# A one-core decode block: the last V loaded earlier, all heads treated alike, the MLP's inner products as rows, and W_down in row blocks

## The chip, the cores and the metric

The kernel runs on one core of one Trainium2 chip. The metric is the device time of one execution in microseconds (us), as a median over several executions. Below, DVE is the vector engine, ACT the scalar engine, PE the matmul engine, PEld its weight loads, POOL the GpSimd engine, and SP the engine that issues most DMA transfers.

A profile shows one execution. Its span runs from the first to the last instruction and is about 2 us shorter than the device time of the same execution. Times within a profile are us from the span's start.

## The reference, cut to what matters

Two rows of 512 numbers go through a layer norm, an attention block with one query per row against a cache, a residual, another layer norm and a gated MLP with a residual.

```
x: 2 x 1 x 512      K, V cache: 2 x 32 heads x 8192 x 128 (bf16)
q = layernorm(x) @ wq;  p = softmax(q . K / sqrt(128));  o = p @ V
h  = x + o @ wo                                  # wo: 4096 x 512
n  = layernorm(h)
y  = h + (relu(n @ W_gate) * (n @ W_up)) @ W_down   # F = 1376
```

The cache is 268 MB of the 281 MB that the kernel reads, and each byte of it is used once.

## The kernel before: the parts that matter

Four heads make a quad. There are 16 quads; quad 15 is the last. DVE multiplies K by the query and adds up the products, ACT takes the exponentials, and PE multiplies the weights by V. K has two buffers, V has one. After the loop, all remaining weights go into the K buffer that quad 14 leaves:

```python
for n in range(N - 1):
    scores(n, ...)
    if n + 2 < N: load_k(n + 2)
    collect(); ...; weighted_v(n)
    if n + 2 < N: load_v(n + 1)
W = kring.tile([P, RING], bf16, tag="k", name="W")
# ... cut: wo_sb, wol, wgu, wd_sb are views of W
for k, n in enumerate(SIZES): ...                # load wo
CUTS = (0, T // 2, T * 7 // 8, T * 15 // 16, T)
load_v(N - 1, CUTS)                              # then the last V
# ... then gate, up, W_down in blocks of 128 rows, and 96 rows last
```

The last quad takes a road of its own. The first seven eighths of its V are summed as rows and the last eighth as columns (`v_stationary`). Its sums come out as columns (one head after another), go into a small multiply, and join the rest of the attention row, which has been multiplied by `wo` beforehand:

```python
o_sum = lanes_of(o15)                            # DVE: four masked steps
v_stationary(N - 1, o_b, CUTS[2], CUTS[3])
nc.tensor.matmul(out=o_b, lhsT=o_sum, rhs=lane_of[:, 0, :], ...)
v_stationary(N - 1, o_b, CUTS[3], T)
normalize_last(L, o_b, zil)
for h in range(G):
    project(wol[:, h, :], ol[:, h, :], last=(h == G - 1))
hc = a_ps + xc                                   # (as code: one DVE add)
mu = centred(hc, "ln2");  hd = hc - mu           # (shortened)
mlp_in(0, gate_ps)       # 44 matmuls of 2 columns: the weights are loaded, hd moves
var = variance(hd_f, "ln2")
mlp_in(1, up_ps)         # 44 more
# ... cut: relu, product; then 44 matmuls of 128 columns with W_down; y_row; two output DMAs
```

The softmax here doesn't subtract the row's maximum and nothing guards it: scores larger than these inputs give would overflow.

Of the kernel before, what the change touches and what calls it, by code (L numbers as in the profile page):

```python
# [17 lines left out]
def kernel(  # L18
# [13 lines left out]
    nc = tc.nc  # L32
# [38 lines left out]
    zm = consts.tile([P, B, NQ - 1], f32)  # L71
    zl = consts.tile([P, B, G], f32)
# [6 lines left out]
    nc.vector.memset(eps_t, EPS)  # L79
    nc.vector.memset(mean_c, 1.0 / D)  # L80
    nc.vector.memset(zm, 0.0)
    nc.vector.memset(zl, 0.0)
    nc.vector.memset(row_of, 0.0)
    ident = consts.tile([P, P], bf16)
    masks.make_identity(nc, ident)
    zero = consts.tile([P, 1], bf16)
    nc.gpsimd.memset(zero, 0.0)
    nc.gpsimd.memset(pm, 0.0)

    SIZES = (4, 2, 1)  # L90
    FIRST = (0, 4, 6)
# [3 lines left out]
    half_blk = consts.tile([P, 2], f32)  # L95
    pick = {n: consts.tile([P, Q // n], f32, name=f"pick{n}") for n in SIZES}
    spread = {n: consts.tile([P, min(n, 2), G, Q // n], f32, name=f"spread{n}") for n in SIZES}
    same = {n: consts.tile([P, n, G, Q // n], f32, name=f"same{n}") for n in SIZES}

    def build_masks():  # L100
        def red(out, in_, axis=AXIS.X):
            nc.vector.tensor_reduce(out=out, in_=in_, axis=axis, op=ALU.add)

        red(turn_of, ident.rearrange("p (g t h) -> p t g h", t=TG, h=G), AXIS.XY)
        red(lane_of, ident.rearrange("p (g u t h) -> p u h g t", u=2, t=TG, h=G), AXIS.XY)
        red(head_blk, ident.rearrange("p (h m) -> p h m", h=G))
        red(half_blk, ident.rearrange("p (u m) -> p u m", u=2))
        red(row_of[:, 0:B], ident.rearrange("p (g q) -> p q g", q=Q)[:, 0:B, :])
        for n in SIZES:
            u = min(n, 2)  # L110
            red(pick[n], ident.rearrange("p (h m) -> p m h", m=Q // n))
            nc.vector.tensor_copy(spread[n], _view(lane_of, 0, [[G, u], [1, G], [0, Q // n]]))
            nc.vector.tensor_copy(same[n], _view(head_blk, 0, [[0, n], [1, G], [0, Q // n]]))
# [7 lines left out]
    x_row = opool.tile([B, D], bf16, tag="row")  # L121
# [6 lines left out]
    def centred(hc, pfx):  # L128
# [5 lines left out]
        return mu.unsqueeze(1).to_broadcast([P, KC, B])  # L134
# [13 lines left out]
    for c in range(KC):  # L148
# [5 lines left out]
    nc.vector.tensor_tensor(out=xd, in0=xc, in1=centred(xc, "ln1"), op=ALU.subtract)  # L154
# [3 lines left out]
    xn = misc.tile([P, KC, B], bf16)  # L158
    nc.vector.tensor_tensor(out=xn, in0=xd, in1=rstd.unsqueeze(1).to_broadcast([P, KC, B]),
                            op=ALU.mult)  # L160
    xnb = opool.tile([P, KC, B, Q], bf16, tag="row")
    nc.vector.tensor_copy(xnb, xn.unsqueeze(3).to_broadcast([P, KC, B, Q]))
    nc.scalar.activation(out=warm, in_=xn[0:1, 0, 0:1], func=ACT.Exp)
# [3 lines left out]
    qrep = consts.tile([P, B, NQ, Dh], bf16)  # L167
# [25 lines left out]
    LQ = NQ - 1  # L193
# [21 lines left out]
    def scores(n, cuts=(0, T)):  # L215
# [4 lines left out]
        for lo, hi in zip(cuts[:-1], cuts[1:]):  # L220
# [10 lines left out]
            nc.vector.tensor_reduce(out=sc[:, lo:hi], in_=kp[:, :, 0:8], axis=AXIS.X, op=ALU.add)  # L231
        for h in range(G):
            ps = slice(h * Q, (h + 1) * Q)
            nc.scalar.activation(out=p_of[ps, :, :, h],  # L234
                                 in_=sc[ps, :].rearrange("p (g t) -> p g t", t=TG), func=ACT.Exp,
                                 accum_out=(zm[ps, b, i:i + 1] if i < LQ else zl[ps, b, h:h + 1]),
                                 scale=SCALE)
# [3 lines left out]
    NK = sum(SIZES) * J  # L241
    oc = misc.tile([P, NK, B], bf16)
    ol = misc.tile([P, G, B], bf16)
    ou = misc.tile([P, NK], f32)
    reps, pair = {}, {}

    def clear(o):

        nc.tensor.matmul(out=o, lhsT=_view(zero, 0, [[0, P]]), rhs=_view(zero, 0, [[0, TG * Dh]]),
                         start=True, stop=False, skip_group_check=True)  # L250
# [12 lines left out]
    def lanes_of(o):  # L263

        osb = opool.tile([P, Dh], f32, tag="row", name="osb")
        nc.vector.tensor_scalar_mul(osb, o[:, 0:Dh], turn_of[:, 0:1])  # L266
        for t in range(1, TG):
            nc.vector.scalar_tensor_tensor(out=osb, in0=o[:, t * Dh:(t + 1) * Dh],  # L268
                                           scalar=turn_of[:, t:t + 1], in1=osb,
                                           op0=ALU.mult, op1=ALU.add)  # L270
        return osb

    def place(i):
        k = max(a for a in range(len(SIZES)) if FIRST[a] <= i)
        return k, i - FIRST[k]

    def weighted_v(n):
        b, i = seq[n]
        k, u = place(i) if i < LQ else (None, 0)
        paired = i < LQ and SIZES[k] > 1  # L280
        if not paired or u % 2 == 0:
            pair["o"] = ps_o.tile([P, TG * Dh], f32, tag="o", name="o")
        o = pair["o"]
        lane = u % 2 if paired else 0
        done = lane == 1 or not paired
        v_moving(n, o, 0, T, lane, first=(lane == 0), last=done)
        pair["done"] = (o, b, i) if done else None

    def collect():

        if not pair.get("done"):
            return
        o, b, i = pair.pop("done")
        osb = lanes_of(o)
        if i == LQ:
            o_l = ps_s.tile([P, G], f32, tag="st", name="o_l")
            nc.tensor.matmul(out=o_l, lhsT=osb, rhs=lane_of[:, 0, :], start=True, stop=True)  # L297
            nc.vector.tensor_copy(ol_f, o_l)  # L298
            return
        k, u = place(i)  # L300
        where = 0 if k == 0 else 1
        if u // 2 == 0 and k < 2:
            reps[where] = ps_acc.tile([P, 2, Dh], f32, tag=f"rep{where}", name="rep")
        n_of = SIZES[k]
        at = (u // 2) * 2 * (P // n_of)
        m = min(n_of, 2) * (P // n_of)
        nc.tensor.matmul(out=reps[where][at:at + m, max(k - 1, 0), :],  # L307
                         lhsT=spread[n_of].rearrange("k u h m -> k (u h m)"),
                         rhs=osb, start=True, stop=True, skip_group_check=True)

    def gather(k):

        n_of = SIZES[k]
        j, m = J * n_of, Q // n_of
        r = reps[0 if k == 0 else 1][:, max(k - 1, 0), :]
        at = FIRST[k] * J
        nc.vector.tensor_tensor(out=r.rearrange("p (m j) -> p m j", j=j),  # L317
                                in0=r.rearrange("p (m j) -> p m j", j=j),
                                in1=_view(pick[n_of], 0, [[1, m], [0, j]]), op=ALU.mult)
        nc.vector.tensor_reduce(out=ou[:, at:at + j], in_=r.rearrange("p (m j) -> p j m", j=j),  # L320
                                axis=AXIS.X, op=ALU.add)

    def v_stationary(n, o, lo, hi):
        vt = vts[n]
        for t in range(lo, hi):
            nc.tensor.matmul(out=o, lhsT=vt[:, t, :], rhs=p_of[:, t // TG, t % TG, :],
                             start=(t == CUTS[2]), stop=(t == T - 1), skip_group_check=True)

    def sum_z(zb, lhsT, z):
        nc.tensor.matmul(out=zb, lhsT=lhsT, rhs=z, start=True, stop=True)  # L330
        return zb

    def row_z(b, zb):
        for k, n in enumerate(SIZES):
            sum_z(zb[:, FIRST[k]:FIRST[k] + n], same[n].rearrange("p u h m -> p (u h m)"),
                  zm[:, b, FIRST[k]:FIRST[k] + n])
        return zb

    def last_z(b, zb):

        return sum_z(zb, mean_f, zl[:, b])

    def z_tile():
        return ps_s.tile([P, LQ + G], f32, tag="st", name="zb")

    def normalize(b, zb):
        zs = misc.tile([P, 6], f32, name=f"zs{b}")
        nc.vector.tensor_tensor(out=zs[:, 0:4], in0=zb[:, 0:4], in1=head_blk, op=ALU.mult)
        nc.vector.tensor_tensor(out=zs[:, 4:6], in0=zb[:, 4:6], in1=half_blk, op=ALU.mult)
        zi = misc.tile([P, 3], f32, name=f"zi{b}")  # L350
        nc.vector.tensor_reduce(out=zi[:, 0:1], in_=zs[:, 0:4], axis=AXIS.X, op=ALU.add)
        nc.vector.tensor_reduce(out=zi[:, 1:2], in_=zs[:, 4:6], axis=AXIS.X, op=ALU.add)
        nc.vector.tensor_copy(zi[:, 2:3], zb[:, 6:7])
        nc.vector.reciprocal(out=zi, in_=zi)
        for k, n in enumerate(SIZES):
            at = FIRST[k] * J
            nc.vector.tensor_scalar_mul(oc[:, at:at + n * J, b], ou[:, at:at + n * J],  # L357
                                        zi[:, k:k + 1])

    def invert_last(b, zb):  # L360
        zi = misc.tile([P, G], f32, name=f"zil{b}")
        nc.vector.reciprocal(out=zi, in_=zb)
        return zi

    def normalize_last(b, o, zi):
        nc.vector.scalar_tensor_tensor(out=ol[:, :, b], in0=o, scalar=1.0 / D,
# [202 lines left out]
```

## Time and profile before

| what | value | where it is read |
|---|---|---|
| time | 661.11 us (three runs, 661.11 to 661.63) | timed runs |
| DVE busy | 609.6 us of 659.4 (92%) | page, part 1 |
| HBM read | 281.06 MB, 426 GB/s over the span | page, part 3 |
| scores of quad 15 end | 631.86 | chain of waits |
| V's row sums (its first seven eighths) taken up | 645.75 | timeline |
| last V matmul (of the last eighth) ends | 648.12 | timeline |
| centred row `hd` starts | 650.12 | timeline |
| y matmuls start; y_row starts | 654.38; 656.09 | timeline |

These lines are from the page of the kernel before: busy time by engine, then for 40 equal slices of the span the DMA engines' busy share in tenths (9 is 90% or more) and the GB/s moved.

```profile
PE 119.5 (18%) x1341; PEld 58.6 (9%) x1341; DVE 609.6 (92%) x225; ACT 55.8 (8%) x142; POOL 2.5 (0%) x8
...
DMA  9999999999999999999999999999999999999996
GB/s 382 445 445 445 395 433 446 437 445 418 417 445 437 441 442 398 445 445 426 441 417 433 445 422 441 437 417 441 426 441 441 421 438 426 433 441 433 393 420 259
```

The DMA engines are busy for 90% or more of every slice but the last. DVE is nearly as long. So the body is a stream. That leaves the tail after the last scores. The chain of waits for it, followed back from the last instruction (start, duration, engine, tile written, source line):

```profile
629.57 2.29 DVE sc L231
...
639.53 2.49 PE o L257 x32
...
644.34 1.31 PE o L257 x24
...
650.12 0.17 DVE hd L493
...
654.38 1.17 PE y_ps L466 x31
...
656.09 0.29 DVE y_row L535
```

There is no DMA in this chain, in the pieces that are cut here either: from 631.86 to 656.09, 24.23 us, the tail is bound by compute. The traffic meanwhile ends earlier, as the windows of 1 us show (length; busy time and count on PE, PEld, DVE, ACT and POOL; granted PE clock as a share of full speed; DMA share; GB/s; a transfer's packet is counted in the window in which it starts, so a share can pass 1):

```profile
651.00:652.00 1.00, 1.00 (x30) 1.00 (x28) 0.00 (x0) 0.00 (x0) 0.00 (x0) 0.50 1.06 425
652.00:653.00 1.00, 1.00 (x23) 1.00 (x23) 0.42 (x4) 0.00 (x0) 0.00 (x0) 0.50 0.90 320
653.00:654.00 1.00, 1.00 (x29) 0.97 (x27) 0.15 (x2) 0.00 (x0) 0.00 (x0) 0.50 0.51 166
654.00:655.00 1.00, 0.67 (x21) 0.45 (x24) 0.24 (x2) 0.00 (x0) 0.00 (x0) 0.50 0.08 30
```

### The profile page before, as it was taken

How to read it: one execution, taken by the hardware profiler on the slowest of the kernel's cores; microseconds unless marked ns; L12 is line 12 of the kernel's file. 1: busy time of each engine (PE TensorE's matmuls, PEld its weight loads, DVE VectorE, ACT ScalarE, POOL GpSimd, SP SyncE). 2: the span in 40 equal slices, each digit the busy share in tenths (PEclk: the TensorE clock that was granted, in tenths of full speed). 3: DMA queues.
4: the chain of work that ended last, by engine and by line, in shares of the span. 5: the costliest groups of instructions: out<-in, count | busy, mean ns of one | idle time of the engine just before them, and what ended most of it. 6: DMA issues, size and time to landing. Idle time of an engine off the chain costs nothing.

```text
span 659.4 us, 3234 instructions
## 1 busy us (share of the span) xinstructions
PE 119.5 (18%) x1341; PEld 58.6 (9%) x1341; DVE 609.6 (92%) x225; ACT 55.8 (8%) x142; POOL 2.5 (0%) x8
## 2 busy tenths in 40 slices
PE   2100302003030210303012130301202030020446
PEld 1000101001010100101001110100001010010225
DVE  2899999999999999999999999999999998999952
ACT  2201001010101001010101001010010101001020
POOL 1000000000000000000000000000000000000000
PEclk9555755757565575756557575555757555575656
DMA  9999999999999999999999999999999999999996
GB/s 382 445 445 445 395 433 446 437 445 418 417 445 437 441 442 398 445 445 426 441 417 433 445 422 441 437 417 441 426 441 441 421 438 426 433 441 433 393 420 259
DMA packets 7314, 281.26 MB, mean 427 GB/s; under 512 B 802, under 2 KB 1412, under 8 KB 2308
## 3 DMA queue, kind: packets, MB, share of 16 engines
q1 hardware_dynamic: 7272, 281.06, 98.9%
q8 instruction: 10, 0.16, 0.1%
q14 instruction: 4, 0.03, 0.0%
q10 hardware_dynamic: 28, 0.01, 0.0%
HBM read 281.06 MB, written 0.00 MB: 426 GB/s over the span
## 4 chain that ended last, share of the span: by engine, by line
DVE 62%; DMA 33%; PE 3%; issue 1%; ACT 0%; DVEq 0%
DMA k<-in_A_k_cache_dram 31%; DVE k L222 29%; DVE k L228 28%; DVE sc L231 4%; DMA wq_sb<-in_A_wq_dram 2%; DVE osb L268 1%; DVE qrep L188 1%; PE qps L175 1%; PE o L257 1%; PE ar_ps L452 0%; ACT qrep L186 0%; PE y_ps L466 0%; PE a_ps L459 0%; PE gate_ps L510 0%; PE up_ps L510 0%
## 5 line engine op out<-in xcount | busy, mean ns | idle before, releaser
L222 DVE TENSOR_TENSOR k<-k,qrep 128x32768 bf16<-128x32768 bf16 (+1 forms) x17 | 275.7, 16217 | 8.9 <-DMA k<-in_A_k_cache_dram 8.8
L228 DVE TENSOR_TENSOR k<-k 128x16384 bf16<-128x16384 bf16 (+3 forms) x68 | 266.8, 3923 | 2.3
L257 PE MATMUL o<-v,pm 128*32 128x512 bf16 x1016 | 88.1, 522 | 395.8 <-DMA v<-in_A_v_cache_dram 395.8
L234 ACT ACTIVATE pm<-sc 32x256 bf16<-32x256 f32 x64 | 47.2, 738 | 563.9 <-DVE sc L231 527.6
L257 PEld LDWEIGHTS <-pm 128*32 128x32 bf16 x1016 | 37.9, 127 | 444.8 <-issue 282.3
L231 DVE TENSOR_REDUCE sc<-k 128x256 f32<-128x2048 bf16 (+1 forms) x17 | 36.7, 2161 | 1.6
L307 PE MATMUL rep<-osb,spread 128*64 128x128 f32 (+1 forms) x16 | 5.9, 474 | 110.5 <-DVE osb L268 110.5
L234 ACT ACTIVATION_READ_ACCUMULATOR pm<-sc 32x1 f32 x64 | 15.0, 234 | 0.0
L307 PEld LDWEIGHTS rep<-osb,spread 128*64 128x64 f32 (+1 forms) x16 | 3.2, 257 | 114.1 <-DVE osb L268 114.1
L188 DVE CAST qrep<-qps 32x512 bf16<-32x512 f32 x8 | 5.5, 692 | 7.2 <-ACT qrep L186 7.1
L266 DVE TENSOR_SCALAR osb<-o,turn_of 128x128 f32<-128x128 f32 x10 | 3.4, 344 | 9.2 <-PE o L257 9.2
L268 DVE SCALAR_TENSOR_TENSOR osb<-o,turn_of,osb 128x128 f32<-128x128 f32 x30 | 10.5, 351 | 1.1
L175 PE MATMUL qps<-wq_sb,xnb 128*64 128x512 bf16 x32 | 6.5, 562 | 7.0 <-DMA wq_sb<-in_A_wq_dram 4.8
L186 ACT ACTIVATE qrep<-qps 32x512 bf16<-32x512 f32 x8 | 4.7, 586 | 8.5 <-PE qps L175 5.2
L152 DVE COPY xc<-x_ps 128x8 f32<-128x8 f32 x1 | 0.2, 167 | 4.9 <-PE x_ps L149 4.9
L510 PEld LDWEIGHTS <-W 128*128 128x128 bf16 (+1 forms) x88 | 3.8, 126 | 0.3 <-issue 0.3
L175 PEld LDWEIGHTS <-xnb 128*64 128x64 bf16 x32 | 2.7, 147 | 10.0 <-issue 5.3
L452 PE MATMUL ar_ps<-W,oc 128*2 128x512 bf16 x28 | 3.2, 626 | 1.8 <-DVE oc L357 1.8
L297 PE MATMUL o_l<-lane_of,osb 128*128 128x4 f32 x2 | 0.6, 364 | 12.8 <-DVE osb L268 12.8
L317 DVE TENSOR_TENSOR rep<-rep,pick 128x128 f32<-128x128 f32 x6 | 1.8, 295 | 1.0 <-PE rep L307 0.9
L330 PE MATMUL zb<-zm,same 128*128 128x4 f32 (+2 forms) x12 | 2.3, 306 | 0.3 <-DVE ol_f L298 0.3
L330 PEld LDWEIGHTS zb<-zm,same 128*128 128x128 f32 x12 | 2.1, 258 | 0.8 <-issue 0.4
(92 smaller groups left out, 44.3 us busy)
## 6 DMA issues: line engine op xcount, KB each, us to landing
k<-in_A_k_cache_dram SPq DMA_DIRECT2D x2, 4096.0 KB
wq_sb<-in_A_wq_dram SPq DMA_DIRECT2D x1, 4096.0 KB, 12.3
v<-in_A_v_cache_dram SPq DMA_DIRECT2D x1, 4096.0 KB, 13.3
v<-in_A_v_cache_dram SPq DMA_DIRECT2D x1, 3072.0 KB, 20.2
W<-in_A_wo_dram SPq DMA_DIRECT2D x1, 2048.0 KB
W<-in_B_W_gate_dram SPq DMA_DIRECT2D x1, 1376.0 KB
W<-in_B_W_up_dram SPq DMA_DIRECT2D x1, 1032.0 KB, 27.4
W<-in_A_wo_dram SPq DMA_DIRECT2D x1, 1024.0 KB, 29.0
```

The lines of the kernel that those rows point to most:

```text
L175: nc.tensor.matmul(out=qps[h * B * Q:(h + 1) * B * Q], lhsT=xnb[:, c].rearrange("p b q -> p (b q)"), rhs=wq_v[:, c, g:g + QP, h0 + h, :], ...
L186: nc.scalar.activation(out=dst, in_=src, func=ACT.Copy)
L188: nc.vector.tensor_copy(dst, src)
L222: nc.vector.tensor_tensor(out=kp, in0=kp, in1=_view(qrep[:, b, i, :], 0, [[0, hi - lo], [1, Dh]]), op=ALU.mult)
L228: nc.vector.tensor_tensor(out=kp[:, :, 0:half], in0=kp[:, :, 0:half], in1=kp[:, :, half:width], op=ALU.add)
L231: nc.vector.tensor_reduce(out=sc[:, lo:hi], in_=kp[:, :, 0:8], axis=AXIS.X, op=ALU.add)
L234: nc.scalar.activation(out=p_of[ps, :, :, h], in_=sc[ps, :].rearrange("p (g t) -> p g t", t=TG), func=ACT.Exp, accum_out=(zm[ps, b, i:i + ...
L257: nc.tensor.matmul(out=o[g:g + W2], lhsT=_view(pm, (0 if lane else R) + t // TG * W2, [[1, W2]]), rhs=vt[:, t:t + TG, :].rearrange("p t d ...
L268: nc.vector.scalar_tensor_tensor(out=osb, in0=o[:, t * Dh:(t + 1) * Dh], scalar=turn_of[:, t:t + 1], in1=osb, op0=ALU.mult, op1=ALU.add)
L307: nc.tensor.matmul(out=reps[where][at:at + m, max(k - 1, 0), :], lhsT=spread[n_of].rearrange("k u h m -> k (u h m)"), rhs=osb, start=True, ...
L330: nc.tensor.matmul(out=zb, lhsT=lhsT, rhs=z, start=True, stop=True)
L510: nc.tensor.matmul(out=ps[0:w, fc, :], lhsT=lhsT, rhs=hd[:, c, :], start=(c == 0 and fc == 0), stop=(c == KC - 1), skip_group_check=True)
```

## The change

The intent is to finish V earlier and to simplify. V of quad 14 comes in halves, so that the single V buffer can be refilled half by half: the last V follows directly, and `wo` comes after it. All quads go the same way in groups of four, so the last quad's columns, masks and small multiplies vanish. Gate and up are computed as rows (24 matmuls of 512 columns instead of 88 of two, three of them side by side), and four small matmuls turn the activations back. W_down comes in blocks of 128, 104 and 112 rows, one to a partition; each such row holds four rows of W_down, 4 KB.

The diff, cut to its core (cuts marked with `...`; masks, layer-norm helpers and renaming left out):

```diff
+            load_v(n + 1, (0, T) if n + 3 < N else HALVES)
 ...
+    vts[L] = vts[L - 1]
+    CUTS = (0, T // 2, T * 7 // 8, T)
+    for lo, hi in zip(HALVES[:-1], HALVES[1:]):
+        weighted_v(L - 1, lo, hi)
+        for a, b in zip(CUTS[:-1], CUTS[1:]):
+            if lo <= a < hi:
+                load_part(vts[L], A_v_cache, L, a, b)
+    for k in range(NGR):
+        load_wo(k)
+    scores(L)
+    X = kring.tile([P, RING], bf16, tag="k", name="X")     # gate, up, W_down: the buffer of K 15
+    ROWS = (P, 104, F // RD - P - 104)
+    ends = [RD * sum(ROWS[:j + 1]) for j in range(FT)]
+    offs = [e - MT for e in ends]
 ...
+        rows = B_W_down[ends[j] - RD * ROWS[j]:ends[j], :].rearrange("(p r) n -> p r n", r=RD)
+        for r0, r1 in ((0, RD),) if j < FT - 1 else ((0, RD - 1), (RD - 1, RD)):
+            nc.sync.dma_start(out=wd_sb[P - ROWS[j]:, j, r0:r1], in_=rows[:, r0:r1])
 ...
     def lanes_of(o):
-        osb = opool.tile([P, Dh], f32, tag="row", name="osb")
-        nc.vector.tensor_scalar_mul(osb, o[:, 0:Dh], turn_of[:, 0:1])
-        for t in range(1, TG): ...                          # three more masked adds
+        om = ...    # one masked product over 512 columns
+        osb = ...   # one reduction of 512 columns to 128
 ...
+    attention_rows(0, NK - JG)                              # 16 matmuls with wo
+    for lo, hi in zip(CUTS[1:-1], CUTS[2:]):
+        weighted_v(L, lo, hi)
+    collect()
+    gather()
+    normalize(B - 1, NGR - 1)
+    attention_rows(NK - JG, NK)                             # the last 16
+    nc.scalar.activation(out=ar, in_=ar_ps, func=ACT.Copy)
+    for c in range(KC):                                     # turned to columns, fp32
+        nc.tensor.matmul(out=h_ps[:, c, :], lhsT=ar..., rhs=row_of[:, 0:B], ...)
-                nc.tensor.matmul(out=ps[0:w, fc, :], lhsT=lhsT, rhs=hd[:, c, :], ...)   # x88
+                nc.tensor.matmul(out=ps[j * Q:(j + 1) * Q, :], lhsT=hd[:, c]...,
+                                 rhs=wgu[:, g, c, offs[j]:offs[j] + MT], ...)           # x24
```

## The prediction

Some of its words: "lanes" is picking, from the 512 columns of V's sums, the 128 that belong to each partition; "rep" or "spread" is a small matmul that puts them on the right partitions; "gather" brings them to the columns that `wo` takes. "Exp" is the exponentials, "ar" the attention row. Its times are the ends of steps.

> **What bounds the kernel now.** The page gives 281.26 MB moved at a mean 427 GB/s, the DMA row at 9 in nearly every slice. DVE is nearly as long (92% busy; one quad is 17.2 + 8.7 + 4.4 + 2.3 + 1.2 + 2.3 = 36.1 us in the chain of waits, one quad of K and V at the 435 GB/s of the middle slices is an estimated 38.5 us). K of the last quad lands at 595.5, its scores end at 631.9. From there the chain is no longer DMA: 24.5 us of PE, DVE and ACT until y_row (656.1 to 656.4), then 3 us of output and end. DMA traffic ends near 653.6 (windows of 1 us), so the tail is bound by compute, by about 2 us.
>
> **What does not change.** The order of transfers up to K of quad 15, the score arithmetic, the q stage (bound by wq landing at 13.0). I expect the scores of quad 15 to end at 632 +/- 1 again. Fewer DVE instructions are worth nothing: DVE waits for K in the last quads. Only the tail counts.
>
> **Transfers after.** V14 lands in halves (about 605 and 615), the first half of V15 is issued near 609 and the queue never empties: V15 lands by 634 (now 643 to 644), wo by 639 and 644 (now 624), gate and up by 650, W_down by 653.5, as now.
>
> **The tail, summed (us).** Exp ends 635.0 (four of 0.98). First V15 half: 32 matmuls at half clock, 3.2 (64 took 6.33 for quad 14) -> 638.3. x matmul 0.4; wait for wo to 639.1; 16 wo matmuls 1.7 -> 640.8. Rest of V15: 32 matmuls, 2.4 (clock partly full) -> 643.3. Lanes: one 512-wide product and one reduction, estimated 0.7 each from 0.29 for 128 columns and 0.69 for a 512-wide cast; rep 0.85; gather 0.65; normalize 0.25 -> 646.5. Last 16 wo matmuls 1.4, copy 0.7, four fp32 transposing matmuls 2.0, mean and hd 1.1 -> 651.8. y of ar 0.35; gate 12 matmuls in threes, 1.75; var 0.4; up 1.75 -> 656.0. act 0.75, four transposes 0.35, copy 0.2, 48 y matmuls 1.9, y_row 0.3 -> 659.5, against 656.4.
>
> So V finishes about 2 us earlier (643.3 against 645.6), but the way from there to hd is 8.4 us instead of 4.7 (the last quad now goes the lane, spread, gather road, and the whole of ar waits for it), and hd to y_row is 7.6 instead of 6.1. Net: about 3 us lost.
>
> **Clock.** The skill, "TensorE: Matmul & The Clock Gate", section "What's actually happening", says activity releases the throttle; the windows agree (half at 636.4, full at 641 to 647.7, half again). I assume the MLP runs at half clock.
>
> **Prediction.** 663.5 us, 8 in 10 between 660.3 and 666.5. Chances: faster by over 2% 0.01, within 2% 0.98, slower by over 2% 0.01.
>
> **What would show it.** V15's first matmuls at about 635; V done near 643; hd near 652; PE, not DMA, ending the idle times after 645; the stream's end unmoved near 653.5.
>
> **What would make it wrong.** A stream shortened by dropping the 1 KB rows of wo, if K15 comes earlier; full clock through the MLP (saves about 2); V14's halves leaving the queue empty (costs its gap only if scores shift or wo lands late).

## The result, and the profile after

The changed kernel took 662.71 us (six runs, 661.84 to 663.82) against 661.11 us before (six runs, 660.92 to 661.68). The ratio of the fast runs (after over before) is 1.0024, with a 95% interval of 1.0011 to 1.0037: slower by about 1.6 us. Ratios here are the mean time of one kernel's fast runs over the mean of the other's fast runs of the same rounds, so they are not quite the ratio of the medians quoted.

The page of the changed kernel, same lines as above:

```profile
PE 115.3 (17%) x1211; PEld 50.3 (8%) x1211; DVE 606.1 (92%) x162; ACT 56.1 (8%) x143; POOL 6.7 (1%) x15
...
DMA  9999989999999999999999999999999999999996
GB/s 381 444 444 444 437 388 440 444 444 441 440 392 440 440 441 436 444 404 437 436 440 440 440 409 440 432 436 440 437 428 428 436 425 440 440 412 431 429 417 190
```

PE and DVE have fewer instructions (ACT has one more, POOL seven), and DVE saves 3.5 us of work, but the stream is as long as it was. The last slice differs: 190 GB/s instead of 259. The tail, from the timeline (start, us, engine, line, operation, tiles and shapes, count, and in brackets the idle time before it with what ended it):

```profile
629.45 2.29 DVE L221 TENSOR_REDUCE sc<-k 128x256 f32<-128x2048 bf16 x1
...
642.60 0.69 DVE L251 TENSOR_TENSOR om<-o,turn_of 128x512 f32<-128x512 f32 x1 [6.00 <-PE o L242]
643.33 1.02 DVE L255 TENSOR_REDUCE osb<-om 128x128 f32<-128x512 f32 x1
...
647.56 2.03 PE L407 MATMUL h_ps<-row_of,ar 128*128 128x2 f32 x8 [0.70 <-ACT ar L403]
...
650.54 0.29 DVE L414 TENSOR_TENSOR hd<-hc,ln2mu 128x128 bf16<-128x128 f32 x1 [0.75 <-PE ln2mu L126]
...
655.78 0.39 PE L430 MATMUL y_ps<-X,act_t 128*2 128x128 bf16 x16 [0.28 <-DVE act_t L467]
657.03 0.30 PEld L430 LDWEIGHTS <-act_t 128*2 128x2 bf16 x16 [1.05 <-DMA X<-in_B_W_down_dram]
657.04 1.30 PE L430 MATMUL y_ps<-X,act_t 128*2 128x128 bf16 x32 [0.86 <-DMA X<-in_B_W_down_dram]
657.74 0.38 PEld L430 LDWEIGHTS <-act_t 128*2 128x2 bf16 x16 [0.40 <-DMA X<-in_B_W_down_dram]
658.39 0.29 DVE L473 CAST y_row<-y_ps 128x128 bf16<-128x128 f32 x1 [2.66 <-PE y_ps L430]
```

The scores end at the same time as before. V's sums are taken up 3.2 us earlier (and the last V matmul, at 648.12 before, is done 5.5 us earlier), `hd` is 0.4 us later, and at the end PE waits for W_down, twice. The windows say why:

```profile
651.00:652.00 1.00, 1.00 (x12) 0.34 (x9) 0.66 (x2) 0.00 (x0) 0.00 (x0) 0.50 0.93 218
652.00:653.00 1.00, 1.00 (x8) 0.29 (x2) 0.00 (x0) 0.00 (x0) 0.00 (x0) 0.50 1.07 232
653.00:654.00 1.00, 1.00 (x11) 0.50 (x13) 0.70 (x3) 0.00 (x0) 0.00 (x0) 0.66 0.84 142
654.00:655.00 1.00, 0.41 (x6) 0.00 (x0) 0.90 (x2) 0.00 (x0) 0.00 (x0) 1.00 0.64 121
```

In the first two of these windows the DMA engines are as busy as before (share 0.93 and 1.07) but move 218 and 232 GB/s instead of 425 and 320. Busy engines with fewer bytes are the sign to look for: it is not a lack of work but slow transfers. The packet list in the stored traces says the same: here a 4 KB packet took 159 ns at the median in the window at 649, and 338 and 279 ns at 650 and 651; in the kernel before it took 159 and 161 ns at 650 and 651.

The four pieces of the tail, as differences of starts in the two profiles (us):

| piece | before | after | difference |
|---|---|---|---|
| scores end to V's sums taken up | 631.86 to 645.75 = 13.89 | 631.74 to 642.60 = 10.86 | -3.03 |
| from there to `hd` | to 650.12 = 4.37 | to 650.54 = 7.94 | +3.57 |
| from there to the first y matmul | to 654.38 = 4.26 | to 655.78 = 5.24 | +0.98 |
| y matmuls until y_row | to 656.09 = 1.71 | to 658.39 = 2.61 | +0.90 |
| sum | 24.23 | 26.65 | +2.42 |

The first two rows of the table need care. Before, the last eighth of V is still multiplied in the second piece, until 648.12. Counted up to the last V matmul, the first piece would have got about 5.4 us shorter and the second about 6 us longer. Only their sum, +0.54 us, does not depend on where the cut is made.

The profiled execution of the changed kernel took 663.46 us, 0.75 us above its median, which is most of the difference between 2.42 and 1.6.

### The profile page after: what moved, and what is told of

Same layout as the page of the kernel before. It is cut to its first block, busy times and chain, and to the rows that moved or that the text cites. A ratio compares the mean times of both kernels' runs of the same rounds, so it can differ in the third digit from the quotient of the medians.

```text
span 661.6 us, 2916 instructions
## 1 busy us (share of the span) xinstructions
PE 115.3 (17%) x1211; PEld 50.3 (8%) x1211; DVE 606.1 (92%) x162; ACT 56.1 (8%) x143; POOL 6.7 (1%) x15
## 4 chain that ended last, share of the span: by engine, by line
DMA 85%; PE 13%; DVE 0%; ACT 0%; issue 0%; SPq 0%
DMA v<-in_A_v_cache_dram 80%; PE o L242 12%; DMA X<-in_B_W_down_dram 4%; DMA wq_sb<-in_A_wq_dram 2%; PE qps L166 1%; DVE qrep L179 0%; ACT qrep L177 0%; PE y_ps L430 0%; SPq L190 0%; DVE y_row L473 0%
## 5 line engine op out<-in xcount | busy, mean ns | idle before, releaser
L242 PE MATMUL o<-v,pm 128*32 128x512 bf16 x1024 | 89.7, 525 | 404.6 <-DMA v<-in_A_v_cache_dram 404.6
L221 DVE TENSOR_REDUCE sc<-k 128x256 f32<-128x2048 bf16 x16 | 36.6, 2285 | 2.0 <-DVE k L218 0.5
L283 PE MATMUL rep<-osb,spread 128*64 128x128 f32 x16 | 5.1, 421 | 104.9 <-DVE osb L255 104.9
L251 DVE TENSOR_TENSOR om<-o,turn_of 128x512 f32<-128x512 f32 x8 | 5.5, 683 | 6.0 <-PE o L242 6.0
L283 PEld LDWEIGHTS rep<-osb,spread 128*64 128x64 f32 x16 | 2.2, 196 | 108.7 <-issue 62.1
L369 POOL MEMSET X<- 24x2048 bf16 (+1 forms) x2 | 3.5, 1794 | 621.6 <-DVE sc L221 621.6
L255 DVE TENSOR_REDUCE osb<-om 128x128 f32<-128x512 f32 x8 | 8.2, 1023 | 0.3
```

Source lines behind the costliest of these rows:

```text
L221: nc.vector.tensor_reduce(out=sc, in_=kt[:, :, 0:8], axis=AXIS.X, op=ALU.add)
L242: nc.tensor.matmul(out=o[g:g + W2], lhsT=_view(pm, (0 if lane else R) + t // TG * W2, [[1, W2]]), rhs=vt[:, t:t + TG, :].rearrange("p t d ...
L251: nc.vector.tensor_tensor(out=om.rearrange("p (t d) -> p t d", d=Dh), in0=o.rearrange("p (t d) -> p t d", d=Dh), in1=_view(turn_of, 0, [[1 ...
L255: nc.vector.tensor_reduce(out=osb, in_=om.rearrange("p (t d) -> p d t", d=Dh), axis=AXIS.X, op=ALU.add)
L283: nc.tensor.matmul(out=state["rep"][u * m:(u + 1) * m, :], lhsT=spread.rearrange("k u h m -> k (u h m)"), rhs=osb, start=True, stop=True, ...
L369: nc.gpsimd.memset(wd_sb[0:P - ROWS[j], j], 0.0)
```

## The experiments

My theory of the time: the earlier V is worth about 3 us, and the longer road from V to the MLP and the slow W_down eat it. My theory of W_down, called A below: blocks that miss some of the 128 partitions are slow to load. Its rivals were the streaming matmuls (B), the split of the last block (C) and chance (N).

The first four ran on one chip, beside nine runs of the kernel before with a median of 661.42 us.

**after_again.** The changed kernel, unedited.

> The changed kernel once more, unedited, for a second trace and a firmer time. Theory A (the rows of W_down that miss some partitions, 104 and 112 of 128, make their transfers slow): traffic falls to near 220 GB/s from about 650 us again and the last W_down piece is waited for until about 657.7. Rival N (chance: contention in that one execution): traffic stays near 400 GB/s to 653 and no wait for W_down is seen. Time 661.8 to 663.8 under A, near 661.4 under N.

Measured: 662.77 us (five runs), ratio 1.0019 (1.0005 to 1.0033). The traffic fell to 282, 199 and 232 GB/s in the three windows from 650 on, and PE waited for the last W_down piece until 657.55. So N falls, and the half rate belongs to this kernel.

**wd128.** Each W_down block as 128 rows. The rows that a block shares with its neighbour are loaded twice, and masked in the activations instead of in W_down.

```diff
-            nc.gpsimd.memset(wd_sb[0:P - ROWS[j], j], 0.0)
+            nc.gpsimd.memset(own[0:P - ROWS[j], j:j + 1], 0.0)      # own: ones elsewhere
-        rows = B_W_down[ends[j] - RD * ROWS[j]:ends[j], :]...
+        rows = B_W_down[offs[j]:ends[j], :]...
-            nc.sync.dma_start(out=wd_sb[P - ROWS[j]:, j, r0:r1], in_=rows[:, r0:r1])
+            nc.sync.dma_start(out=wd_sb[:, j, r0:r1], in_=rows[:, r0:r1])
-    nc.vector.tensor_copy(act_t, act_ps)
+    nc.vector.tensor_tensor(out=act_t, in0=act_ps, in1=(own, broadcast), op=ALU.mult)
```

> Each of the three W_down blocks is loaded as all 128 rows (16 and 24 rows twice, 0.16 MB more, an estimated 0.4 us at 430 GB/s), and the doubled rows are masked in the activations. Theory A: traffic stays near 400 GB/s to the end, W_down lands by about 654, the y matmuls run straight after the activations at 655.8, and the time falls by about 1.2 us against the changed kernel, to about 661.4. Rival B (the gate and up matmuls that stream the same buffer slow the transfers) and rival C (the split of the last block in 3 KB and 1 KB) and N each expect no change of the landing: 657.7 or later, time unchanged or 0.4 us longer.

Measured: 662.38 us (five runs), ratio 1.0015 (1.0003 to 1.0028). Windows of its profile:

```profile
651.00:652.00 1.00, 1.00 (x14) 0.35 (x15) 0.89 (x4) 0.00 (x0) 0.00 (x0) 0.50 1.04 405
652.00:653.00 1.00, 1.00 (x9) 0.15 (x3) 0.19 (x1) 0.00 (x0) 0.00 (x0) 0.50 0.83 321
653.00:654.00 1.00, 1.00 (x8) 0.53 (x8) 0.24 (x2) 0.00 (x0) 0.00 (x0) 0.50 0.52 196
654.00:655.00 1.00, 1.00 (x12) 0.27 (x6) 0.81 (x2) 0.00 (x0) 0.00 (x0) 0.77 0.11 41
```

More bytes, and yet the transfers are through 2 us earlier. All 48 y matmuls ran in one piece of 0.84 us with no wait for a DMA, and y_row started at 657.39. B and C are both still in this kernel (the gate and up matmuls stream the same buffer, and the last block is still split), so neither makes the half rate without the partial blocks. The size was a miss: I expected 1.2 us off the time, and the median fell by 0.4 us, with overlapping intervals. The profile says why: the activations themselves came at 656.49 here, so the wait for W_down hid a chain that was close behind it.

**wo_first.** `wo` loaded before the last V again, all else as in the changed kernel.

```diff
+    for k in range(NGR):
+        load_wo(k)
     for lo, hi in zip(HALVES[:-1], HALVES[1:]):
         weighted_v(L - 1, lo, hi)
         ...
-    for k in range(NGR):
-        load_wo(k)
```

> One part undone: wo is loaded before the last V, as in the kernel before. My theory of the tail: V15 then lands at about 644 instead of 634, its last matmuls wait for it and end near 646 instead of 642.6, and all after it shifts by 3 to 3.5 us: y_row near 661 and the time 665 to 666. Rival (the order is worth nothing because W_down's late landing at 657.7 is what ends the kernel): time within 1 us of the changed kernel, 662 to 663.5.

Measured: 665.16 us (five runs), ratio 1.0059 (1.0046 to 1.0072), 2.4 us above after_again. The last eight V matmuls waited for their DMA until 644.07:

```profile
644.07 0.61 PE L242 MATMUL o<-v,pm 128*32 128x512 bf16 x8 [1.00 <-DMA v<-in_A_v_cache_dram]
```

After that, V's sums were taken up at 644.73, and y_row started at 660.20. The W_down half rate was there too and cost nothing, as the activations came at 659.30. So the new order is worth about 2.4 us to this kernel. It is the one part of the change that is shown to pay; the others were not undone one by one.

**thin_mlp.** Gate and up take one chunk of four (a wrong result).

```diff
-    mlp_in(0, gate_ps)
+    mlp_in(0, gate_ps, 0, 1)
-    mlp_in(1, up_ps)
+    mlp_in(1, up_ps, 0, 1)
```

> Wrong result on purpose: gate and up take only the first of four chunks, so 6 wide matmuls instead of 24 stream the weight buffer while W_down lands. Theory A: the traffic from 650 us stays near 220 GB/s, W_down's end near 657.7, so the time stays within 0.5 us of the changed kernel although the activations are ready about 2 us earlier. Rival B (the streaming matmuls slow the transfers): traffic recovers to near 400 GB/s, W_down lands near 654 and the time falls by 2 to 3 us.

Measured: 662.86 us (four runs), ratio 1.0020 (1.0007 to 1.0034). The activations were ready at 654.89, 1.9 us before those of after_again (656.75), and the time did not move: PE waited for W_down until 656.58 and again until 657.28. Traffic was 209, 230 and 236 GB/s from 650 on, with a quarter of the streaming matmuls. This refutes B a second time, and it shows that W_down's landing bounds the changed kernel as soon as the chain is quicker.

The next five ask what exactly is slow about the blocks. Each was run once with a profile, on wd128 as the base, and none is meant to be faster.

**wd_104** and **wd_112.** Only the second block partial (104 rows at partitions 24 to 127), or only the third (112 rows at 16 to 127).

```diff
+    part = 1                                    # wd_112: part = 2
+    lead = [P - ROWS[j] if j == part else 0 for j in range(FT)]
+    nc.gpsimd.memset(wd_sb[0:lead[part], part], 0.0)
-        rows = B_W_down[offs[j]:ends[j], :]...
+        rows = B_W_down[offs[j] + RD * lead[j]:ends[j], :]...
-            nc.sync.dma_start(out=wd_sb[:, j, r0:r1], ...)
+            nc.sync.dma_start(out=wd_sb[lead[j]:, j, r0:r1], ...)
```

> Only the second W_down block stays partial (104 rows at partitions 24 to 127), the first and third are loaded as 128 rows. If the 104 rows [...]are the slow ones: traffic falls to near 220 GB/s from about 650.5, at the end of the first block, and recovers when they are through; W_down lands near 656. If only the 112 rows of the third block are slow: traffic near 400 GB/s to 653 as with three full blocks.

> Only the third W_down block stays partial (112 rows at partitions 16 to 127[...]). If the 112 rows are slow: near 400 GB/s until about 651.5, then about half, landing near 656. If only the 104 rows are slow: near 400 GB/s to 653, as with three full blocks.

Measured: with the 104 rows, 202 and 220 GB/s in the windows at 651 and 652 (405 and 321 with full blocks), 662.87 us. With the 112 rows, 353 at 651 and then 206 at 652 and at 653, 663.23 us. Both are slow, each from about where its block begins. One part of the expectation failed: after the 104 rows the rate did not recover, although the third block is whole in this kernel:

```profile
653.00:654.00 1.00, 1.00 (x11) 0.66 (x11) 0.36 (x3) 0.00 (x0) 0.00 (x0) 0.50 0.94 192
654.00:655.00 1.00, 0.85 (x12) 0.12 (x6) 0.80 (x2) 0.00 (x0) 0.00 (x0) 0.90 0.77 173
```

The packet list shows it too. Only the third block has packets of 3 KB. They took 224, 280 and 212 ns at the median in the windows 652 to 654, and 130 ns at 655, when three 4 KB packets were left; in wd128 they took 125 ns at 652 and 653. So a whole block beside a partial one is slowed with it: what is slow is the stretch in which they run together, not the partial transfer alone.

**wd_104_low.** The 104 rows at partitions 0 to 103.

```diff
+    offs[1] = ends[0]
+    # memsets: own is 1 in rows 0..103 of column 1; wd_sb[:, 1] cleared first
+            nc.sync.dma_start(out=wd_sb[0:(ROWS[1] if j == 1 else P), j, r0:r1], ...)
```

> The second block again 104 rows, but at partitions 0 to 103[...]; the others are full. If the shift against the partitions is the cause: the traffic stays[...] and W_down lands by about 654.5. If [...]a row count under 128, are the cause: half rate again, landing near 656 as with 104 rows at 24 to 127.

Measured: 230, 212 and 215 GB/s in the windows from 651 on, 662.95 us. So moving the rows to the low partitions does not help. My idea that a shift against the neighbouring blocks does it falls.

**wd_64_64** and **wd_96_32.** The second block whole, the same bytes to the same places as in wd128, but as two transfers.

```diff
+            for p0, p1 in ((0, 64), (64, P)) if j == 1 else ((0, P),):     # 96 in wd_96_32
+                nc.sync.dma_start(out=wd_sb[p0:p1, j, r0:r1], in_=rows[p0:p1, r0:r1])
```

> The second W_down block is loaded whole, but by two transfers of 64 rows. If any transfer of fewer than 128 rows, or engines that serve other partitions than in the blocks around, halves the rate: traffic near 220 GB/s from about 651 as with 104 rows. If it takes a row count that is no power of two, or a count that 16 engines do not share evenly: near 400 GB/s to 653 as with three full blocks.

> The second W_down block whole, by transfers of 96 and 32 rows (both a multiple of 16). If a row count that is no power of two is the cause: near half rate from about 651. If only an uneven share over 16 engines is (104 rows): near 400 GB/s to 653. The 112 rows[...] fell to about 206 GB/s at 652 to 654 and speak for the first.

Measured: 248, 255 and 219 GB/s with 64 and 64 rows in the windows from 651 on (663.41 us), 206, 255 and 218 with 96 and 32 (663.77 us). These lines are from wd_64_64; set them against the first two of wd128 above:

```profile
651.00:652.00 1.00, 1.00 (x17) 0.35 (x12) 0.85 (x4) 0.00 (x0) 0.00 (x0) 0.50 1.07 248
652.00:653.00 1.00, 1.00 (x10) 0.16 (x4) 0.00 (x0) 0.00 (x0) 0.00 (x0) 0.50 1.01 255
```

The same source, the same destination and the same bytes, cut once across the partitions, run at 248 instead of 405 GB/s. So it is neither the addresses nor a row count that is no power of two. One transfer more is not it either: up comes in two, over 128 partitions, ahead of W_down, and this same profile shows no drop there (418 GB/s in the window at 649). In every one of these experiments with a W_down block that spans fewer than 128 partitions, the traffic from that block on fell to about half. One case in the traces differs: the last W_down block of the kernel before is 96 rows of 1 KB (96 KB in all), and its packets took 46 ns at the median, as the 1 KB packets of whole blocks did in wd128. So a small partial block at the end of the stream is not shown to be slow.

The Trainium skill has this, on a page that I did not look up for the prediction. "SBUF — State Buffer", section "Door 1: The DMA port swizzle", says that DMA bandwidth depends on how many of 16 ports the partitions of a transfer reach, and that 64 partitions from 0 reach 8. Its section "Can I just issue two DMAs to hit both halves?" says: "The only way to hit all 16 ports is one transfer spanning all 128 partitions." The 64 and 64 rows agree (248 GB/s against 405). By the page's table the 104 and 112 rows reach all 16 ports, and yet they fell to 202 and 206, so the second sentence fits these rates better than the table does, and the count of ports reached is not the whole of it. Which ports were used, and why a whole block beside a partial one is slow too, is open: the traces give no engine and no port for a transfer's parts.

**short_h.** wd128, with the attention row turned to columns in bf16 and the y matmuls of that row moved behind gate.

```diff
-    nc.scalar.activation(out=ar, in_=ar_ps, func=ACT.Copy)          # fp32
+    nc.scalar.activation(out=ar_b, in_=ar_ps, func=ACT.Copy)        # bf16
+    nc.vector.tensor_copy(ar, ar_ps)                                # fp32, beside it
-        lhsT=ar..., rhs=row_of[:, 0:B]
+        lhsT=ar_b..., rhs=row_b
-    y_rows(row_of, ar, first=True)
     mlp_in(0, gate_ps)
+    y_rows(row_of, ar, first=True)
```

> On top of the three full W_down blocks: the attention row is copied to bf16 for the four transposing matmuls (DVE makes the fp32 copy beside it), and the y matmuls of that row go behind the gate matmuls. My theory that the road from the last V to the activations is what costs the changed kernel its time: those four fall from 2.0 us to about 0.5, hd comes at about 649.4 instead of 651.0, the activations are ready near 654, y_row starts near 655.7 (then W_down, which lands near 655, bounds it) and the time falls by about 1.6 us against the version with full blocks, to about 660.8. Rival (the stream's end bounds the tail already): no change beyond 0.3 us from 662.4.

Measured: 660.85 us (five runs, beside 661.25 for before), ratio 0.9992 (0.9980 to 1.0005), correct. The four matmuls went from eight passes in 2.03 us to four in 0.29 us. The piece from V's sums to `hd` fell from 7.94 to 6.46 us (641.29 to 647.75). The time came out as expected, but in part by luck: from the end of the scores to y_row it is 24.42 us against 25.42 in wd128, so 1.0 us less, and the scores themselves ended at 630.46 instead of wd128's 631.97, which no edit aimed at (see short_all_again).

**short_all.** As short_h, and the last pair's sums are selected and spread by PE: a bf16 copy halved between ACT and DVE, then four matmuls with masks, in place of product, reduction and two fp32 passes.

```diff
+        nc.scalar.activation(out=ob[:, half:], in_=o[:, half:], func=ACT.Copy)
+        nc.vector.tensor_copy(ob[:, 0:half], o[:, 0:half])
+        for t in range(TG):
+            nc.tensor.matmul(out=state["rep"][...], lhsT=spread_t[:, t, :],
+                             rhs=ob[:, t * Dh:(t + 1) * Dh], start=(t == 0), stop=(t == TG - 1), ...)
```

> As short_h, and the last pair's lanes are selected and spread by four bf16 matmuls from a copy halved between ACT and DVE, instead of a masked product, a reduction (0.69 + 1.02 us) and two fp32 passes. I expect the road from the last V matmul to the gathered row to shrink by about 1.2 us, hd near 648.2, the activations ready near 653; W_down then bounds the end, y_row near 655.4 and the time about 660.4, so at most 0.5 us better than short_h and about 1 us better than the kernel before. Rival (PE clock phase, not the road, set the tail): no ordered difference between the two.

Measured: 659.69 us (five runs), ratio 0.9980 (0.9966 to 0.9994), correct. It is faster than the kernel before by 1.6 us in the medians (1.3 us by the ratio), and than the changed kernel by about 3 us. The timeline of its profile:

```profile
628.15 2.29 DVE L229 TENSOR_REDUCE sc<-k 128x256 f32<-128x2048 bf16 x1
...
640.89 0.42 DVE L305 CAST ob<-o 128x256 bf16<-128x256 f32 x1 [5.60 <-ACT ob L304]
641.37 0.38 PE L307 MATMUL rep<-ob,spread_t 128*64 128x128 bf16 x4 [0.94 <-DVE ob L305]
...
644.48 0.29 PE L434 MATMUL h_ps<-row_b,ar_b 128*128 128x2 bf16 x4 [0.70 <-ACT ar_b L428]
...
645.97 0.29 DVE L441 TENSOR_TENSOR hd<-hc,ln2mu 128x128 bf16<-128x128 f32 x1 [0.75 <-PE ln2mu L133]
...
654.49 0.29 DVE L501 CAST y_row<-y_ps 128x128 bf16<-128x128 f32 x1 [1.60 <-PE y_ps L457]
```

From V's sums (ACT takes up its half at 640.48) to `hd` is now 5.49 us instead of 7.94. The tail from the end of the scores (630.44) to y_row is 24.05 us, against 26.65 in the changed kernel and 24.23 in the kernel before. So the tail is only level with the kernel before. The gain over it comes from somewhere else: the scores end 1.4 us earlier. I had edited nothing there except two small mask tiles and some buffer assignments. And the road that got shorter did not shorten the tail as much: up waited 0.57 us for its own DMA, and the 48 y matmuls took 1.50 us at clock 0.50 (0.84 in short_h). The median is 1.2 us below short_h, where I had expected 0.5 at most, with overlapping intervals.

**short_all_again.** The same once more, on another chip, to see whether that is a matter of the chip.

> short_all once more, unedited, because in both traces of the short versions the scores of the last quad ended 1.2 us earlier (630.4 us) than in all ten traces of the others (631.6 to 632.0), before any edited instruction of the tail. If that belongs to the kernel: scores end near 630.4 again. If it was the chip or the execution: 631.6 to 632. In both cases I expect y_row 24.0 us after that, 2.3 us less than in the changed kernel, and a ratio to the kernel before of 0.997 to 0.9995.

Measured: 659.90 us (five runs, beside 661.31 for before), ratio 0.9978 (0.9965 to 0.9992). The scores ended at 630.33, and y_row started 24.56 us later (24.0 expected; short_h had 24.42, so the tail of short_all is not shown to be shorter than that of short_h). So the earlier end of the scores belongs to the kernel: it is in all three traces of the short versions, on two chips, and in none of the other eleven. None of the other edited versions was profiled on these two chips, but the kernel before took the same time on all four chips of the experiments (medians 661.25 to 661.42), which speaks against the chip. The product with K started at 284.87 for quad 7 and at 594.05 for quad 15 in short_all, 0.9 us and 1.3 us earlier than in the changed kernel (285.73 and 595.36). In between that is 38.65 us a quad against 38.70. The stream itself is faster by a hair, early and late. Why is open: the memory that the tiles get is one thing that differs, and no run separates it.

## Why the prediction was right, and where it was wrong

The time was right: 663.5 us predicted, 662.71 measured, inside the range, and slower by about the amount (2.4 predicted against 661.11, 1.6 measured). The range, 660.3 to 666.5, also holds the time of the kernel before, so being inside it says little. The steps are the test; they fared unequally, and two errors partly cancelled, so that the total came this close is luck.

- **Right: the body does not move.** Predicted end of the scores 632 +/- 1, measured 631.74 (631.86 before). DVE's 3.5 us less work bought nothing, since it waits for K.
- **Right: V ends about 2 us earlier.** Predicted 643.3, measured 642.60 and 643.26 in two traces (3.2 and 2.5 us before 645.75); exp ended at 634.9 (635.0 predicted). wo_first shows by experiment that the order makes most of it (644.73 with the old order). What the prediction calls V's end before, 645.6, is that of the first seven eighths; the last V matmul ended at 648.12.
- **Right, 0.2 us too long: the road from V to `hd`.** Predicted 8.4 instead of 4.7, to the end of `hd`. Measured 8.23 instead of 4.54 (to its start, as in the table, 7.94 instead of 4.37), so the loss of 3.7 us was put at 3.7. One term was low: the reduction took 1.02 us and I had put 0.7. The Trainium skill, "VectorE: DVE Perf Modes", section "Rules for kernel authors", calls `tensor_reduce` the slowest DVE op; here it took 1.02 us for the same 512 columns that the product took 0.69 us for. Other terms were high: the last 16 wo matmuls took 1.03 us at full clock, not 1.4.
- **Wrong: "gate and up by 650, W_down by 653.5, as now", in what it says of W_down.** The step took for granted that 104 and 112 rows load like 128. PE waited for W_down until 657.7, and the rate from 650 on was about half. wd128, with more bytes and full rows, brings back 405 GB/s.
- **Wrong with it: "PE, not DMA, ending the idle times after 645" and "the stream's end unmoved".** The last two groups of y matmuls waited for a DMA.
- **Wrong size: the MLP.** Predicted 7.6 us from the end of `hd` to the end of y_row. Measured 7.85 in the first trace, but with the wait for W_down in it; in wd128, without that wait, 6.35. The main term was the y matmuls: where W_down was not in the way (wd128) the 48 took 0.84 us, not 1.9. I had assumed half clock throughout; the windows show full clock from 654 to 657 in the changed kernel's profile. The Trainium skill, "TensorE: Matmul & The Clock Gate", section "What's actually happening", says that recent activity sets the clock. These traces agree that it comes and goes within the tail, and that one tail is not like the next: in short_all the same 48 matmuls took 1.50 us at clock 0.50. A sum at one fixed clock is off by up to a microsecond here.

So the chain was predicted about 2 us too slow (an estimate: activations at 655.78 and 656.75 in the two traces, plus the 0.90 and 0.29 us that wd128 needed from there to the end of y_row, make 657.0 and 657.9 instead of 659.5), and W_down too early by about 4 us. W_down then ended the kernel about 1 us before the time that the chain had been given (the end of y_row was predicted at 659.5 and measured at 658.68 and 658.42).

In the changed kernel the gain of the order (2.4 us in the time, by wo_first) is spent on the uniform road from V to `hd` (+3.57 us by the profiles; short_h and short_all take 2.4 us of it back), on the MLP as rows (+0.98 us from `hd` to the first y matmul) and on W_down's landing (2.61 us for the last piece, where wd128 needs 0.90; the medians show 0.4 us of that, inside the noise). The order's gain is shown by a run that undoes it. The other amounts are read from profiles: no run undoes the uniform road as a whole or the MLP as rows.

## What to carry to other kernels

When a DMA stream bounds the body, less compute in the body buys nothing. The time changes only with the stream itself (as in the short versions, by 1.4 us and for no reason found) or with what comes after the last dependent transfer, and there the length of the dependent chain counts, not the number of instructions: a uniform road that is cheaper in total can be longer for the last piece. Try transfers that span all 128 partitions, even at the price of loading some rows twice and masking them (here 405 GB/s instead of 218 in the window at 651, though only 0.4 us of time, inside the noise), and look for a DMA share near 1 with half the GB/s as the sign of slow transfers. A wait at the very end can hide a chain right behind it, so removing the wait is worth only the difference.

## What the Trainium skill lacked or had wrong

- "SBUF — State Buffer", section "Door 1: The DMA port swizzle", counts the ports that the partitions reach. By its table, partitions 24 to 127, 16 to 127 and 0 to 103 all reach 16 ports, yet the traffic fell to 202 (window at 651), 206 and 212 GB/s (at 652), where whole blocks had 405 and 321. The sentence of the section "Can I just issue two DMAs to hit both halves?", that only one transfer over all 128 hits all ports, fits better. The page lacks a figure for transfers of 65 to 127 partitions, and one for what they cost a whole transfer beside them (3 KB packets of a whole block: 280 ns instead of 125 in the window at 653).
- "DMA: Bandwidth & Descriptors", section "Why a DMA increments its semaphore by 16 and not by 1", gives 16 engines to transfers whose row count divides by 16. A reader could take that for full rate; 112 rows ran at 206 GB/s and 64 and 64 rows at 248. That section lacks a pointer to the port rule.
- No page that I read explains a stream that is steadily a little faster in three traces of two versions of a kernel (the last scores ending at 630.3 to 630.5 instead of 631.6 to 632.0 us).
